# Second MLP of a three-stage kernel: when the next span's block sums are formed, in what pieces they are split, and where the common sum is added

## Chip, cores and metric

One core of a Trainium2 chip. The metric is the device time of one execution in microseconds; where several executions of a kernel are compared, their median is taken.

## What is computed

Attention over a packed set of keys, then two MLPs on 4,608 tokens of 512 features; the change is in the second MLP alone. Cut to that:

```python
def _moe2_ref(x, w_in, w_out):          # x 4608 x 512, w_in 512 x 2048, w_out 2048 x 512
    h = x @ w_in
    g = h * (1.0 / (1.0 + np.exp(-1.702 * h)))
    return (g @ w_out).astype(np.float32)
```

## The kernel before

All matrix products of the second MLP are done in fp32 accuracy by pairs: each operand is split into a high part (a rounded copy, made by ACT) and a low part (operand minus high part, a subtraction on DVE or POOL), and three products stand for one (high x high, high x low, low x high).

**Spans.** The tokens are worked through in five spans: three of 2 x 512 tokens and two of 2 x 384. A span is an up and a down product, each done as a two-by-two block product with seven block products in place of eight (Strassen's scheme in Winograd's form). Its price is sums of blocks. The four blocks of x are b11, b12, b21, b22, each 128 partitions x 2 x 512 (or 384) elements; the block operands of the seven products are b11, t1 = b12 - b11, t2 = b22 - t1, t3 = b22 - b12, b21, b22 and t4 = b21 - t2.

**Groups and steps.** The hidden features of a span are worked in four groups; a group has 14 up steps (two halves of seven, in the order a11, s1, s2, s3, a12, s4, a22, with the x operands b11, t1, t2, t3, b21, b22, t4) and 7 down steps. `up(c)` is an up step: six matmuls into a PSUM bank (line 1051), then the additions that make the activations: `u2` starts as a copy of the a11 product (ACT, line 1062), line 1064 adds the s2 product, line 1066 (called v5 below) adds u2 and the s1 bank, line 1071 adds the s3 product, line 1073 adds u2 to the s4 and the a22 products, and ACT applies the activation (line 1074). There are four banks: a11 and a12 share one (a12 accumulates onto what a11 left), s1 and s4 share one, s3 and a22 share one, s2 has its own. So s4 may be written only when v5 has read the bank, a22 only when line 1071 has, and the next s1 only when line 1073 has taken s4.

`form(d)` makes a down operand: sums of activations on DVE (lines 1087 to 1091), a cast `oh` on ACT (line 1095) and a subtraction `ol` on POOL (line 1096). `down(d)` is a down step: 24 matmuls (18 for 384 tokens) in two parts (line 1122), then additions of the PSUM parts to `acc` or to the common sum `accu` (lines 1147 and 1149). Steps 0 and 1 go to the common sum. In the last group of a span, three quarters of `acc` get the common sum added (line 1153), on POOL, all three behind step 1; the output goes out behind steps 5 and 6.

**Hand-over.** The splits of the x blocks lie in seven tiles with one buffer each. In the last group of a span, behind the second half's product that used a tile last, `prepare` refills it for the next span (called from `up`): a cast on ACT (line 935) and a subtraction (line 936) of the whole block, 1,024 or 768 columns; before or after it the sums of blocks in place, on DVE (lines 1024, 1028, 1029 and 1031). The raw blocks are loaded by `load_x` (line 930) from step 6 of the third group on, into buffers of their own. I call the four changes of span hand-over 1 to 4.

**What sets the order.** The program is written step by step, as above, but a scheduler lays out each engine's queue ahead of time: an instruction may stand earlier than in the text as soon as its operands and buffers are free in the scheduler's own count. Each engine then runs its queue strictly in order, and SP issues the DMAs in order.

## Time and profile before

| | |
|---|---|
| median of 3 executions | 1658.5 us (1656.1 to 1660.7) |
| the profiled execution | 1658.6 us, span 1656.7 us |
| busy: TensorE, DVE, ACT, POOL | 97%, 70%, 52%, 56% of the span |
| matmuls | 10,608 |
| granted clock of TensorE, mean | 0.992 of full speed |

The second MLP takes the part of the span from about 923 us on. TensorE is the engine that the rest serves; the other engines' idle time costs nothing as long as TensorE does not wait for them. The profile names for each idle stretch of an engine what ended it.

### The profile page before, as it was taken

How to read it: one execution, taken by the hardware profiler on the slowest of the kernel's cores; microseconds unless marked ns; L12 is line 12 of the kernel's file. 1: busy time of each engine (PE TensorE's matmuls, PEld its weight loads, DVE VectorE, ACT ScalarE, POOL GpSimd, SP SyncE). 2: the span in 40 equal slices, each digit the busy share in tenths (PEclk: the TensorE clock that was granted, in tenths of full speed). 3: DMA queues.
4: the chain of work that ended last, by engine and by line, in shares of the span. 5: the costliest groups of instructions: out<-in, count | busy, mean ns of one | idle time of the engine just before them, and what ended most of it. 6: DMA issues, size and time to landing. Idle time of an engine off the chain costs nothing.

```text
span 1656.7 us, 29176 instructions
## 1 busy us (share of the span) xinstructions
PE 1611.8 (97%) x10608; PEld 1516.4 (92%) x10608; DVE 1161.9 (70%) x2004; ACT 866.7 (52%) x1771; POOL 928.8 (56%) x744
## 2 busy tenths in 40 slices
PE   7899999999999999999999999999999999999997
PEld 5689998999999999999999889899989999999997
DVE  5788988877768777686886476864585458567564
ACT  4667776666566666665655344434344434434432
POOL 2447777656666557562665266564456446546444
PEclk8999999999999999999999999999999999999999
DMA  9655666584565855465445878676667667887874
GB/s 256 178 163 173 205 189 221 190 254 150 167 204 204 271 186 186 148 207 205 167 177 175 293 259 268 218 245 187 188 207 242 192 186 243 281 250 237 286 222 127
DMA packets 217726, 348.21 MB, mean 210 GB/s; under 512 B 93936, under 2 KB 123632, under 8 KB 211440
## 3 DMA queue, kind: packets, MB, share of 16 engines
q1 hardware_dynamic: 217584, 346.35, 65.1%
q8 instruction: 85, 1.39, 0.3%
q14 instruction: 57, 0.47, 0.1%
HBM read 279.19 MB, written 67.11 MB: 209 GB/s over the span
## 4 chain that ended last, share of the span: by engine, by line
PE 77%; DVE 11%; issue 3%; POOL 3%; DMA 3%; ACT 3%; SPq 0%; POOLq 0%; DVEq 0%; ACTq 0%
PE ps_dn L1122 18%; PE ps_up L1051 18%; PE ps_o L748 15%; PE ps_g L712 13%; PE ps_w L679 3%; PE ps_at L308 3%; PE ps_at L353 2%; PE ps_at L297 2%; PE ps_at L443 2%; DMA vn<-in_v_dram 1%; DVE x_t L936 1%; DVE Wl L684 1%; DVE w L131 1%; POOL Hl L734 0%; DVE between L128 0%
## 5 line engine op out<-in xcount | busy, mean ns | idle before, releaser
L1096 POOL TENSOR_TENSOR ol<-g,oh 128x1024 fp32r<-128x1024 f32 (+1 forms) x120 | 267.2, 2237 | 310.4 <-ACT oh L1095 305.2
L1122 PE MATMUL ps_dn<-wo,oh 128*128 128x256 f32 x2016 | 368.3, 284 | 2.3 <-ACT oh L1095 1.3
L1122 PEld LDWEIGHTS ps_dn<-wo,oh 128*128 128x128 f32 x2016 | 319.9, 192 | 10.2 <-ACT oh L1095 2.0
L748 PE MATMUL ps_o<-Hh,wo 128*128 128x384 f32 x1152 | 321.5, 340 | 2.8 <-ACT Hh L733 1.2
L1122 PE MATMUL ps_dn<-wo,ol 128*128 128x256 f32 x1008 | 278.9, 285 | 3.3 <-POOL ol L1096 3.3
L712 PE MATMUL ps_g<-Aqh,Wh 128*128 128x288 f32 x768 | 232.6, 303 | 6.0 <-DVE th L722 1.5
L712 PE MATMUL ps_g<-Aql,Wh 128*128 128x288 f32 x768 | 226.1, 295 | 0.0
L712 PE MATMUL ps_g<-Aqh,Wl 128*128 128x288 f32 x768 | 225.6, 295 | 0.0
L1051 PE MATMUL ps_up<-x_t,wi 128*128 128x512 f32 (+1 forms) x936 | 215.0, 369 | 7.3 <-DVE g L1073 6.0
L748 PEld LDWEIGHTS ps_o<-Hh,wo 128*128 128x128 f32 x1152 | 210.0, 188 | 8.0 <-ACT Hh L733 2.0
L734 POOL TENSOR_TENSOR Hl<-th,Hh 128x576 fp32r<-128x576 f32 x96 | 139.3, 1452 | 134.4 <-ACT Hh L733 134.1
L748 PE MATMUL ps_o<-Hl,wo 128*128 128x384 f32 x576 | 194.6, 338 | 1.4 <-POOL Hl L734 1.3
L1122 PEld LDWEIGHTS ps_dn<-wo,ol 128*128 128x128 f32 x1008 | 190.7, 193 | 4.4 <-POOL ol L1096 3.7
L1051 PEld LDWEIGHTS ps_up<-x_t,wi 128*128 128x128 f32 x936 | 165.8, 188 | 27.2 <-DVE g L1073 7.1
L684 DVE TENSOR_TENSOR Wl<-ps_w,Wh 64x512 fp32r<-64x512 f32 x192 | 131.7, 686 | 73.1 <-ACT Wh L683 70.6
L1074 ACT ACTIVATE g<-g 128x512 f32<-128x512 f32 (+1 forms) x120 | 70.3, 589 | 206.8 <-DVE g L1071 114.2
L763 POOL TENSOR_TENSOR acc<-acc,add 128x384 f32<-128x384 f32 x135 | 139.0, 1041 | 53.9 <-ACT add L761 52.8
L1095 ACT CAST oh<-g 128x1024 fp32r<-128x1024 f32 (+1 forms) x120 | 113.5, 961 | 103.4 <-PE ps_dn L1122 70.8
L1051 PE MATMUL ps_up<-x_b,wi 128*128 128x512 f32 (+1 forms) x702 | 164.4, 368 | 0.0
L712 PEld LDWEIGHTS ps_g<-Aqh,Wh 128*128 128x128 f32 x768 | 144.0, 188 | 12.0 <-DVE th L722 1.8
L1149 DVE TENSOR_TENSOR acc<-acc,ps_dn 128x512 f32<-128x512 f32 (+1 forms) x160 | 99.2, 630 | 77.9 <-PE ps_dn L1122 73.2
L683 ACT CAST Wh<-ps_w 64x512 fp32r<-64x512 f32 x192 | 111.4, 580 | 78.7 <-PE ps_w L679 46.4
(203 smaller groups left out, 3363.0 us busy)
## 6 DMA issues: line engine op xcount, KB each, us to landing
wo<-wo SPq DMA_DIRECT2D x188, 512.0 KB, 3.9
wi<-wi SPq DMA_DIRECT2D x274, 256.0 KB, 3.7
wg<-wg SPq DMA_DIRECT2D x48, 1024.0 KB, 6.2
raw<-in_moe_w_out_dram SPq DMA_DIRECT2D x28, 512.0 KB, 4.3
wi<-stage SPq DMA_DIRECT2D x24, 512.0 KB, 3.6
wo<-stage SPq DMA_DIRECT2D x24, 512.0 KB, 3.6
x<-acc SPq DMA_DIRECT2D x32, 288.0 KB, 3.4
vn<-in_v_dram SPq DMA_DIRECT2D x16, 512.0 KB, 7.2
```

The lines of the kernel that those rows point to most:

```text
L683: nc.scalar.copy(Wh[rows, :, g], src)
L684: nc.vector.tensor_sub(Wl[rows, :, g], src, fl(Wh[rows, :, g]))
L712: nc.tensor.matmul(ps, st[:, o, g, c * P : (c + 1) * P], mv[:, g, cols], start=n == 0, stop=n == 3 * NG - 1)
L734: nc.gpsimd.tensor_sub(Hl, th, fl(Hh))
L748: nc.tensor.matmul(ps, st[:, m * P : (m + 1) * P], mv[:, cols], start=n == 0, stop=n == 3 * len(ss) - 1)
L763: nc.gpsimd.tensor_add(a, a, t)
L1051: nc.tensor.matmul(o, w[:, y, k], x[:, z, k], start=i == 0 and not go_on, stop=i == 5, skip_group_check=bool(go_on))
L1074: nc.scalar.activation(gf, o if q == "a12" else gf, AF.Gelu_apprx_sigmoid)
L1095: nc.scalar.copy(oh, src)
L1096: nc.gpsimd.tensor_sub(ol, src, fl(oh))
L1122: nc.tensor.matmul(o[:, r], x[:, a, (r0 + r) * P : (r0 + r + 1) * P], w[:, a, y], start=i == 0 and not go_on, stop=i == 6 * m - 1, skip_gr ...
L1149: nc.vector.tensor_add(z, z, o[:, :m])
```

## The change

- `sums` is new. It forms t1 into a tile of its own (`xt`, one buffer), t3 in place of b12, and t2 into two 512-column tiles (tag `w`), at steps given in a table: t1 at step 10 and t3 at step 13 of the third group, t2 at step 2 of the fourth. The fourth sum, t4, stays behind the split of b21.
- `prepare` splits each block in two pieces of 512 (384) columns, cast and subtraction in turn, where it did the whole block at once.
- The three additions of the common sum are behind down steps 2, 3 and 4, one each, and on DVE in the last span.

```diff
@@ -1014,21 +1014,35 @@
                         xr[q] = t[:, :, :n]
                         load_part(xr[q], i0, t0 + k * n, n)
 
-            def prepare(s, q):
+            def sums(s, q):
 
                 if s == len(spans):
                     return
                 n = spans[s][1]
-                b11, b12, b21, b22 = (xr[x] for x in ("b11", "b12", "b21", "b22"))
-                if q == "t2":
-                    nc.vector.tensor_sub(b11, b22, b11)
-                source = {"t1": "b11", "t2": "b11", "t3": "b12", "t4": "b21"}.get(q, q)
-                split_x(q, xr[source], nc.gpsimd if q in ("b11", "b21", "b22") else nc.vector, n)
-                if q == "b11":
-                    nc.vector.tensor_sub(b11, b12, b11)
-                    nc.vector.tensor_sub(b12, b22, b12)
-                elif q == "b21":
-                    nc.vector.tensor_sub(b21, b21, b11)
+                if q == "t1":
+                    xr[q] = wp.tile([P, 2, TH], F32, tag="xt", name="xr", bufs=1)[:, :, :n]
+                    nc.vector.tensor_sub(xr[q], xr["b12"], xr["b11"])
+                elif q == "t3":
+                    nc.vector.tensor_sub(xr["b12"], xr["b22"], xr["b12"])
+                else:
+                    xr[q] = [cv.tile([P, TH], F32, tag="w", name="xr", bufs=2)[:, :n] for _ in range(2)]
+                    for k in range(2):
+                        nc.vector.tensor_sub(xr[q][k], xr["b22"][:, k], xr["t1"][:, k])
+
+            def prepare(s, q):
+
+                if s == len(spans):
+                    return
+                n = spans[s][1]
+                src = xr[{"t3": "b12", "t4": "b21"}.get(q, q)]
+                t = x_tile(q, n)
+                for k in range(2):
+                    part = src[k] if q == "t2" else src[:, k]
+                    nc.scalar.copy(t[:, 0, k], part)
+                    (nc.gpsimd if q[0] == "b" else nc.vector).tensor_sub(t[:, 1, k], part, fl(t[:, 0, k]))
+                if q == "b21":
+                    for k in range(2):
+                        nc.vector.tensor_sub(src[:, k], src[:, k], xr["t2"][k])
 
             g, bank, u2 = {}, {}, {}
 
@@ -1147,10 +1161,10 @@
                         nc.scalar.copy(z, o[:, :m])
                     else:
                         nc.vector.tensor_add(z, z, o[:, :m])
-                if last and j == 1:
-                    for k, c in ((1, 1), (0, 1), (1, 0)):
-                        z = acc[k][:, :per, c * HALF : (c + 1) * HALF]
-                        nc.gpsimd.tensor_add(z, z, acc["u"][:, :per])
+                if last and 2 <= j <= 4:
+                    k, c = ((0, 1), (1, 1), (1, 0))[j - 2]
+                    z = acc[k][:, :per, c * HALF : (c + 1) * HALF]
+                    (nc.vector if s + 1 == len(spans) else nc.gpsimd).tensor_add(z, z, acc["u"][:, :per])
                 if last and j >= 5:
                     k = j - 5
                     for r0, m in parts:
@@ -1163,6 +1177,7 @@
                 load_wi(c)
             for d in range(WOB):
                 load_wo(d)
+            EARLY = {10: "t1", 13: "t3", 16: "t2"}
             form_at, down_at = {}, {}
             for d in range(7 * len(turns)):
                 t, j = divmod(d, 7)
@@ -1175,8 +1190,11 @@
                     load_wi(c + WIB)
                     if c >= 7:
                         next(later, None)
-                    if c % PER == 6 and turns[ups[c][0]][1] == NGR - 2:
-                        load_x(turns[ups[c][0]][0] + 1)
+                    s, at = turns[ups[c][0]][0], (turns[ups[c][0]][1] - NGR + 2) * PER + c % PER
+                    if at == 6:
+                        load_x(s + 1)
+                    elif at in EARLY:
+                        sums(s + 1, EARLY[at])
                 for d in form_at.get(c, ()):
                     form(d)
                 for d in down_at.get(c, ()):
```

Where the instructions stand. First DVE around hand-over 1, from the last sum of the block t4 to the first addition of the next group. `xr` are raw blocks and their sums, `x_t` and `x_b` split blocks, `g` and `s` activations, `u` the tile u2. Before:

```order
L1031 TENSOR_TENSOR xr<-xr 128x1024 [waits Pool_49]
L1073 TENSOR_TENSOR g<-u_13359,ps_up 128x512 [waits PE_49] x2
L1149 TENSOR_TENSOR acc_12402<-acc_12402,ps_dn 128x2x256 [waits PE_49]
L936 TENSOR_TENSOR x_t_13532<-xr,x_t_13532 128x1024 [waits Activation_49]
L1087 TENSOR_TENSOR s_13539<-g 128x1024 [waits Activation_49]
L1149 TENSOR_TENSOR acc_12402<-acc_12402,ps_dn 128x2x256 [waits PE_49]
L1088 TENSOR_TENSOR g<-g 128x1024 [waits DVE_49]
L1089 TENSOR_TENSOR g<-s_13539,g 128x1024 [waits DVE_49,Pool_49]
L1149 TENSOR_TENSOR accu<-accu,ps_dn 128x512 [waits PE_49] x2
L1064 TENSOR_TENSOR u_13586<-u_13586,ps_up 128x512 [waits PE_49,Activation_49]
```

and with the change:

```order
L1024 TENSOR_TENSOR xr<-xr 128x1024 [waits DMAHW7_49,DMAHW1_49,DMAHW0_49]
L1087 TENSOR_TENSOR g<-u_13366,ps_up 128x512 [waits PE_49] x2
L1042 TENSOR_TENSOR x_t_13549<-xr,x_t_13549 128x512 [waits Activation_49] x2
L1163 TENSOR_TENSOR acc_12402<-acc_12402,ps_dn 128x2x256 [waits PE_49]
L1101 TENSOR_TENSOR s_13558<-g 128x1024 [waits Activation_49]
L1163 TENSOR_TENSOR acc_12402<-acc_12402,ps_dn 128x2x256 [waits PE_49]
L1102 TENSOR_TENSOR g<-g 128x1024 [waits DVE_49]
L1103 TENSOR_TENSOR g<-s_13558,g 128x1024 [waits DVE_49,Pool_49]
L1163 TENSOR_TENSOR accu<-accu,ps_dn 128x512 [waits PE_49] x2
L1026 TENSOR_TENSOR xr<-xr 128x1024 [waits DMAHW6_49,DMAHW0_49]
L1030 TENSOR_TENSOR xr<-xr 128x512 x2
L1078 TENSOR_TENSOR u_13605<-u_13605,ps_up 128x512 [waits PE_49,Activation_49]
```

Line 1024 (t1 of the span after next) now stands ahead of line 1087 (1073 before), and line 1026 and the two of line 1030 (its t3 and t2) ahead of line 1078 (1064 before); they wait for block loads of that span. The same holds at hand-overs 2 and 3 (at 3 ahead of line 1103). The block sums of the next span itself are gone from this place.

The sums for hand-over 1 do stand in the third group of the first span, on DVE, second half of the group. Before:

```order
L1064 TENSOR_TENSOR u_12971<-u_12971,ps_up 128x512 [waits PE_49,Activation_49]
L1066 TENSOR_TENSOR g<-u_12971,ps_up 128x512 [waits DVE_49]
L1149 TENSOR_TENSOR acc_12402<-acc_12402,ps_dn 128x2x256 [waits PE_49] x2
L1071 TENSOR_TENSOR g<-g,ps_up 128x512 [waits DVE_49,PE_49]
L1149 TENSOR_TENSOR acc_12401<-acc_12401,ps_dn 128x2x256 [waits PE_49] x2
```

and with the change:

```order
L1078 TENSOR_TENSOR u_12971<-u_12971,ps_up 128x512 [waits PE_49,Activation_49]
L1080 TENSOR_TENSOR g<-u_12971,ps_up 128x512 [waits DVE_49]
L1163 TENSOR_TENSOR acc_12402<-acc_12402,ps_dn 128x2x256 [waits PE_49]
L1024 TENSOR_TENSOR xr<-xr 128x1024 [waits DMAHW6_49,DMAHW7_49,DMAHW4_49,DMAHW3_49]
L1163 TENSOR_TENSOR acc_12402<-acc_12402,ps_dn 128x2x256 [waits PE_49]
L1026 TENSOR_TENSOR xr<-xr 128x1024 [waits DMAHW1_49,DMAHW0_49,DMAHW2_49,DVE_49,Pool_49]
L1030 TENSOR_TENSOR xr<-xr 128x512
L1030 TENSOR_TENSOR xr<-xr 128x512 [waits Pool_49]
L1085 TENSOR_TENSOR g<-g,ps_up 128x512 [waits PE_49]
L1163 TENSOR_TENSOR acc_12401<-acc_12401,ps_dn 128x2x256 [waits PE_49] x2
```

The four subtractions stand between line 1080 and line 1085 (1066 and 1071 before), the first of them behind two block loads, the second behind the third.

Last, POOL at the end of the program. Before:

```order
L1096 TENSOR_TENSOR ol<-g,oh 128x2x384 [waits PE_49,Activation_49] x4
L1096 TENSOR_TENSOR ol<-s_19502,oh 128x2x384 [waits PE_49,Activation_49]
L1096 TENSOR_TENSOR ol<-g,oh 128x2x384 [waits PE_49,Activation_49]
L1153 TENSOR_TENSOR acc_18577<-acc_18577,accu 128x3x256 [waits DMAHW5_49,DMAHW4_49,DVE_49]
L1153 TENSOR_TENSOR acc_18576<-acc_18576,accu 128x3x256 [waits DMAHW1_49,DMAHW0_49]
L1153 TENSOR_TENSOR acc_18577<-acc_18577,accu 128x3x256
L1096 TENSOR_TENSOR ol<-g,oh 128x2x384 [waits PE_49,Activation_49] x2
```

and with the change:

```order
L1110 TENSOR_TENSOR ol<-s_19259,oh 128x2x384 [waits PE_49,Activation_49]
L1110 TENSOR_TENSOR ol<-g,oh 128x2x384 [waits PE_49,Activation_49]
L1110 TENSOR_TENSOR ol<-g,oh 128x2x384 [waits DVE_49,PE_49,Activation_49]
L1110 TENSOR_TENSOR ol<-g,oh 128x2x384 [waits PE_49,Activation_49] x4
L1110 TENSOR_TENSOR ol<-s_19578,oh 128x2x384 [waits PE_49,Activation_49]
L1110 TENSOR_TENSOR ol<-g,oh 128x2x384 [waits PE_49,Activation_49] x3
```

The three additions of line 1153 are gone from POOL's queue; the last two `ol` follow the others at once. On DVE they are line 1167, two of them between the two parts of down step 2's additions, the third ahead of those of step 4:

```order
L1105 TENSOR_TENSOR g<-g 128x2x384 [waits Pool_49]
L1163 TENSOR_TENSOR accu<-accu,ps_dn 128x256 [waits DVE_49,PE_49]
L1163 TENSOR_TENSOR acc_18652<-acc_18652,ps_dn 128x2x256 [waits PE_49]
L1167 TENSOR_TENSOR acc_18652<-acc_18652,accu 128x3x256 [waits DVE_49]
L1167 TENSOR_TENSOR acc_18653<-acc_18653,accu 128x3x256
L1163 TENSOR_TENSOR acc_18652<-acc_18652,ps_dn 128x256 [waits PE_49]
L1163 TENSOR_TENSOR acc_18653<-acc_18653,ps_dn 128x2x256 [waits PE_49]
L1163 TENSOR_TENSOR acc_18653<-acc_18653,ps_dn 128x256 [waits PE_49]
L1167 TENSOR_TENSOR acc_18653<-acc_18653,accu 128x3x256 [waits DVE_49]
L1163 TENSOR_TENSOR acc_18653<-acc_18653,ps_dn 128x2x256 [waits DVE_49,PE_49]
```

## Rows read from the trace of the kernel before

**Rows 1.** The waits of TensorE: who waited for whom, us in total, times, longest.

```profile
PE ps_up L1051 <- DVE g L1073: 6.0, 3, 2.4
```

**Rows 2.** Timeline, hand-over 1: start us, us, engine line op out<-in xcount [idle before <-releaser].

```profile
1046.78 1.23 DVE L1028 TENSOR_TENSOR xr<-xr 128x1024 f32<-128x1024 f32 x1
1047.14 3.13 POOL L1096 TENSOR_TENSOR ol<-g,oh 128x1024 fp32r<-128x1024 f32 x1 [0.40 <-ACT oh L1095]
...
1048.04 3.31 DVE L1029 TENSOR_TENSOR xr<-xr 128x1024 f32<-128x1024 f32 x1
...
1065.97 1.27 DVE L1073 TENSOR_TENSOR g<-u,ps_up 128x512 f32<-128x512 f32 x2
...
1066.70 1.66 PE L1051 MATMUL ps_up<-x_t,wi 128*128 128x512 f32 x6 [2.41 <-DVE g L1073]
```

**Rows 3.** Timeline, first span, third group, its second half.

```profile
1010.26 1.96 SPq L930 DMA_DIRECT2D xr<-x  x4
...
1013.73 0.69 DVE L1071 TENSOR_TENSOR g<-g,ps_up 128x512 f32<-128x512 f32 x1 [0.70 <-PE ps_up L1051]
...
1016.89 2.41 POOL L1096 TENSOR_TENSOR ol<-g,oh 128x1024 fp32r<-128x1024 f32 x1 [5.04 <-ACT oh L1095]
...
1019.15 1.52 PE L1051 MATMUL ps_up<-x_t,wi 128*128 128x512 f32 x6
```

**Rows 4.** The tile of the raw blocks and sums, its loads: issue to landing.

```profile
DMA to landing us min/median/max: 2.6/4.1/7.3
```

**Rows 5.** 512-column subtractions on DVE and POOL, and ACT's cast: ns min/median/max, first and last start.

```profile
L957 DVE TENSOR_TENSOR x_t<-x_t,x_t x6: 684/842/1389, 790.5 to 850.2; 128x512 fp32r<-128x512 f32 x6
...
L906 POOL TENSOR_TENSOR stage<-sums,stage x16: 1284/1292/1568, 360.0 to 1001.4; 128x512 fp32r<-128x512 f32 x16
...
L955 ACT CAST x_t<-x_t x6: 611/614/621, 784.7 to 848.8; 128x512 fp32r<-128x512 f32 x6
```

**Rows 6.** Timeline behind hand-over 1, the next span's first group.

```profile
1070.44 0.94 SPq L930 DMA_DIRECT2D xr<-x  x2
...
1071.95 1.22 DVE L1089 TENSOR_TENSOR g<-s,g 128x1024 f32<-128x1024 f32 x1
...
1073.21 2.00 ACT L1095 CAST oh<-g 128x1024 fp32r<-128x1024 f32 x2 [4.50 <-DVE g L1089]
...
1073.81 1.52 PE L1051 MATMUL ps_up<-x_b,wi 128*128 128x512 f32 x6
1074.29 0.68 DVE L1064 TENSOR_TENSOR u<-u,ps_up 128x512 f32<-128x512 f32 x1
1074.34 4.77 POOL L1096 TENSOR_TENSOR ol<-g,oh 128x1024 fp32r<-128x1024 f32 x2 [9.38 <-ACT oh L1095]
...
1079.07 2.40 POOL L1096 TENSOR_TENSOR ol<-s,oh 128x1024 fp32r<-128x1024 f32 x1
```

**Rows 7.** Timeline, TensorE at hand-overs 2 and 4.

```profile
1226.80 1.42 PE L1051 MATMUL ps_up<-x_t,wi 128*128 128x512 f32 x5 [2.40 <-DVE g L1073]
...
1510.25 0.97 PE L1051 MATMUL ps_up<-x_t,wi 128*128 128x384 f32 x4 [1.18 <-DVE g L1073]
```

**Rows 8.** Timeline of the tail.

```profile
1634.89 2.25 DVE L1091 TENSOR_TENSOR g<-g 128x768 f32<-128x768 f32 x1
...
1638.81 5.42 POOL L1153 TENSOR_TENSOR acc<-acc,accu 128x768 f32<-128x768 f32 x3
...
1646.04 0.58 PE L1122 MATMUL ps_dn<-wo,ol 128*128 128x256 f32 x1 [2.84 <-POOL ol L1096]
```

**Rows 9.** The chain of waits at its end: start us, us, what.

```profile
1646.04 6.31 PE ps_dn L1122 x28
```

**Rows 10.** Busy time by stretch: length, PE to POOL busy (xcount), PEclk, DMA share, GB/s.

```profile
1040.00:1095.00 55.00, 52.59 (x327) 47.20 (x326) 42.62 (x43) 24.15 (x30) 35.28 (x14) 1.00 0.69 218
1638.00:1641.00 3.00, 3.00 (x28) 3.00 (x27) 0.72 (x3) 0.90 (x2) 3.00 (x3) 1.00 0.53 165
1646.00:1649.00 3.00, 2.96 (x14) 2.96 (x15) 0.35 (x1) 0.00 (x0) 1.77 (x1) 0.50 0.00 0
```

## The prediction

> **What bounds the kernel now.** I read the waits of TensorE first, then the timelines around the four hand-overs from one span to the next, then the tail. In the second MLP TensorE hardly waits: 6.0 us in three places on DVE's line 1073 [rows 1], and once for 2.84 us on POOL's `ol` in the tail [rows 8]. So the change can win back those waits and what hangs on them, no more; any new wait of TensorE is paid in full.
>
> The waits on line 1073 come from DVE being late at a hand-over. In hand-over 1, DVE forms the sums and the splits of the next span's blocks. The 1,024-column subtraction takes 1.23 us at 1046.78; the next one takes 3.31 us, because POOL's `ol`, started at 1047.14, sits beside it [rows 2]. The row reads as taking turns: `ol` begins in earnest when the first subtraction ends (1048.0), runs 2.3 us to 1050.3, and only then does the second run its 1.1 us, to 1051.35. Were the two to share evenly, the second would end near 1050.3. The Trainium skill (SBUF — State Buffer, section Who interferes with whom) says the same more strictly: a VectorE instruction with two SBUF inputs and a GpSimd instruction that reads SBUF lock each other out for a whole instruction. I use turns below. DVE reaches line 1073 at 1065.97, and TensorE, which needs that bank for the first `t1` product, starts at 1066.70 after 2.41 us idle [rows 2].
>
> **The change, part by part.** The order of the changed program decides this, and it does not put the sums where the table EARLY names them. For hand-over 1 they stand in the third group. For hand-overs 2 to 4 they stand right after the hand-over before: the buffers are free by then, so `t1` moves ahead of the addition to `g` on which TensorE waits, and `t3` and the two pieces of `t2` ahead of the addition to `u2`.
>
> 1. *Third group of the first span.* The four last block loads go out between 1010.26 and 1012.2 [rows 3]; b12's second piece, near 1011.2, lands 4.1 us later at the median [rows 4], 1015.3. `t1` then ends at 1016.5 and an accumulation at 1017.1. `t3` meets `ol` (1016.89 to 1019.30) [rows 3] and ends at 1020.4; two pieces of `t2`, 0.68 us each alone [rows 5], end near 1021.7, and the addition of s3, which stood at 1013.73, ends near 1022.4. The a22 product writes onto the bank that this addition reads, and stood at 1019.15 [rows 3]; the new order puts five down matmuls (0.6 us) ahead of it. **+2.6**, bounds 0 (all loads landed early) and +3.3.
>
> 2. *Hand-over 1, the old wait.* Out go three subtractions, 1.2, 3.3 and 1.2 us. In come 512-column pieces, 0.68 us on DVE, 1.29 on POOL [rows 5]. In turns: the split of `t3` ends at 1056.4; the first piece of `t4` waits for POOL's second b21 piece (1058.9), ends at 1059.5; an accumulation; the second piece waits for an `ol` (to 1061.9), ends at 1062.5; the next span's `t1`, now in this place, waits for a piece of b22 (1063.7) and ends at 1064.9, where line 1073 stood at 1065.97. **-1.1**, bounds -2.4 (the wait gone) and 0.
>
> 3. *Hand-over 1, a new wait.* Counted on with this 1.1 us: `t4` split to 1067.4, the three sums of the activations to 1072.0, two `accu` additions to 1073.2. Now come `t3`, `t2`, `t2` for the next span, and only then `u2` and the addition v5 behind it. b22's load is queued on SP behind b21's, which waits for the split of `t4`; so its second piece is issued near 1069.8 (1070.44 to 1071.38 before), and lands near 1074. But POOL has three `ol` in a row here: the casts started at 1073.21 when line 1089 was done, and POOL ran from 1074.34 through 1081.47 without a gap [rows 6]. Moved up with DVE they start near 1073.2. In turns: `t3` 1075.5 to 1076.6; `ol`; a piece, 1078.9 to 1079.6; `ol`; a piece, 1081.8 to 1082.4; `u2` 1083.0; v5 1083.6, which ended near 1075.7 before (`u2` began at 1074.29, and two such additions take 0.7 each). TensorE's s4 product goes onto the bank that v5 reads. It is through with what stands ahead of it (b21's product, 1.1 us before the 1073.81 of [rows 6] and 1.4 long, the first matmuls of two down steps, then 20 waiting on `ol`) near 1077.9. **+5.8** on s4, and +0.6 on `ol`. Bounds: +2.4 if `t3` gets in ahead of the first `ol`, +8 if b22 lands after the second `ol` began. By even sharing it would be +1.3.
>
> 4. *Hand-over 2* repeats this with 768-column sums; its old wait is the same 2.40 [rows 7]. Here b22's load is one transfer, landing near the moment DVE is free, so `t3` may get in first: 2.8 us of wait, else 5.6. **-1.1 + 4.5**, bounds -2.4 + 2.8 and 0 + 6.6.
>
> 5. *Hand-over 3.* It had no wait. Its sums stand ahead of line 1103 (1089 before), so what they take (0.95 and two of 0.55 by the columns, 2.1 us) and a wait for b22 delay the casts behind it. **+2**, bounds 0 and +4.
>
> 6. *Hand-over 4* has no next span: the sums are gone and nothing takes their place. Its wait of 1.18 [rows 7] goes: **-1.2**, bounds 0 and -1.6.
>
> 7. *The tail.* POOL's three additions of the common sum, 5.42 us from 1638.81, stand ahead of the last two `ol`; TensorE waits 2.84 us, to 1646.04 [rows 8]. It then runs its last 28 matmuls in 6.31 us [rows 9], at a granted clock of 0.50, the lower of its two levels (1.2 GHz of 2.4), where 28 took 3.00 us at 1.00 [rows 10]. In the new order the additions are DVE's. They take turns with three `ol`, as line 1091 does in its 2.25 us [rows 8] for some 0.9 of work: the first ends at 1639.7, the second at 1642.4. The second part of step 4's bank is freed behind it, 1642.8 where TensorE wants it at 1641.1, 1.7 us of new wait. Steps 4 to 6 then end at 1647.8 instead of 1652.4. **-4.6**, bounds -6.3 (no such wait) and -2.8 (the clock falls all the same).
>
> 8. *The clock after new waits.* After 2.41 us of idling in hand-over 1 the granted clock stayed 1.00; in the tail, after 2.84 us, it was 0.50 [rows 10]. A wait of 5.8 us is over both, so I add what half speed costs for a few us after the resumption: **+2.5** over the two places, bounds 0 and +6. The Trainium skill (TensorE: Matmul & The Clock Gate, section HAM oscillation) has every long enough gap in matmul work paid again in slow matmuls behind it; by that alone all three new waits would pay, near +6, by the row of hand-over 1 none.
>
> Costed at nothing: ACT's copies in halves (0.62 us each [rows 5], a quarter of a microsecond more for each block; the products that need them come seven up steps later, and without that cover it would be 0.25 x 7 at each hand-over) and POOL's additions at the other four ends, no longer in one block of 7 us; TensorE did not wait there.
>
> Sum: 2.6 - 1.1 + 5.8 + 0.6 - 1.1 + 4.5 + 2 - 1.2 - 4.6 + 2.5 = **+10.0**. The profiled execution took 1658.6 us (span 1656.7), 0.1 above the median of 1658.5, so 1668.5.
>
> **The rivals.**
> *The sums ride free.* The scheduler put them there because DVE was idle in its own count. If DVE gets to `t3` before the casts are done and b22 has landed by then, v5 is in time. It hangs on one race: b22's landing (2.6 to 7.3 us in [rows 4]) against the first `ol` of the group. Then terms 1, 3, 5 and 8 are nought, and -1.1 - 1.1 - 1.2 - 4.6 = -8.0: 1650.6; with every wait of [rows 1] gone, about 1647. For it: the row of line 1089 and the casts are only 1.3 us apart, so a little less delay wins the race. Against: three `ol` back to back in [rows 6], and a load that cannot go out before `t4` is split.
> *Small waits.* The new waits stay at their lower bounds (2.4 and 2.8) and the clock does not fall: -1.1 + 2.4 + 0.6 - 1.1 + 2.8 - 1.2 - 4.6 = -2.2, up to +2 with part of term 1: 1656 to 1661. For it: even sharing, which [rows 2] speak against.
> *The change does not do what its words say*: for three of four hand-overs the sums are not in the third group. That is in the forecast already.
>
> **How the numbers follow.** Forecast, new waits dearer than the old: 0.54. Riding free: 0.27. Small waits: 0.19. About 0.3% (5.0 us) is what a measurement can tell from no change. So slower 0.54, same 0.19, faster 0.27. The likeliest case by itself runs from 1663.5 to 1681 (upper bounds of 1, 3, 4 and 8). The range reaches down to the riding case, 1650, and up to 1680.
>
> **What would show it.** Right: TensorE waits of 2 us and more on DVE's line 1080 soon after hand-overs 1 and 2; DVE's lines 1026 and 1030 there at two to three times their own length; a wait on line 1085 in the first span's third group; no wait on POOL in the tail, and full clock to the end. Wrong: no TensorE wait on line 1080, or DVE waiting nowhere for block loads; then the time falls to 1651. If the tail still shows half clock, term 7 is oversized by 1.8.

## The result and the profile after

| | |
|---|---|
| before, median of 6 executions | 1658.58 us (1656.10 to 1661.33) |
| after, median of 6 executions | 1669.47 us (1667.53 to 1671.82) |
| after over before | 1.0066, 95% interval 1.0052 to 1.0080 |
| the profiled execution after | 1668.5 us, span 1666.7 us |
| busy after: TensorE, DVE, ACT, POOL | 97%, 70%, 52%, 56% of the span |

The change made the kernel 10.9 us slower. The shares of busy time are the same as before, to the per cent; what changed is in the waits of TensorE over the second MLP (who waited for whom, us in total, times, longest), which answer to [rows 1] (the list is of all of them but one of 0.7 us at the start):

```profile
PE ps_dn L1136 <- DVE accu L1163: 8.2, 2, 7.5
PE ps_up L1065 <- DVE g L1080: 5.3, 1, 5.3
PE ps_up L1065 <- DVE g L1085: 3.6, 2, 2.3
PE ps_dn L1136 <- ACT oh L1109: 2.3, 2, 1.4
PE ps_dn L1136 <- DVE acc L1163: 1.4, 1, 1.4
PE ps_up L1065 <- DVE g L1087: 1.1, 2, 0.7
PE ps_dn L1136 <- POOL ol L1110: 1.0, 2, 0.6
```

The old wait, 6.0 us on line 1073, is down to 1.1 us (line 1087 now). In its place stand one of 7.5 us on an addition to the common sum (hand-over 2), one of 5.3 us on v5 (line 1080, hand-over 1) and one of 2.3 us on line 1085 (third group of the first span). The second wait in four of these groups stood before the change too: 0.8 us on the common sum, 0.9 on `oh` and 0.4 on `ol` in the tail, and 1.3 us on the addition of s3 near 955 us.

To see where the time went, I take one instruction that both kernels run 80 times, DVE's addition of u2 to g (line 1073 before, 1087 after), and compare the starts of the same one in the two profiled executions:

| stretch, from and to a start of that addition before / after | forecast | measured |
|---|---|---|
| all ahead of the change's first place: to 1002.49 / 1000.17 | 0 | -2.3 |
| third group of the first span: to 1041.85 / 1042.15 | +2.6 | +2.6 |
| hand-over 1: to 1119.24 / 1125.58 | +6.6 | +6.0 |
| hand-over 2: from 1201.96 / 1208.31 to 1300.22 / 1314.82 | +4.7 | +8.3 |
| hand-over 3: to 1431.98 / 1448.01 | +2.0 | +1.4 |
| hand-over 4: to 1565.41 / 1579.24 | -1.2 | -2.2 |
| tail: from 1625.72 / 1639.54 to the span's end | -4.6 | -3.8 |
| sum | +10.0 | +10.0 |

(The forecast's 2.5 us for the clock are shared out evenly over hand-overs 1 and 2; the rows are rounded.) The first row is no effect of the change, whose queues are the same up to there: at the same addition the other kernels below stood between 4.7 us earlier and 1.4 us later than before's.

*Third group*, timeline (start us, us, engine line op, idle before and its releaser):

```profile
1013.49 1.23 DVE L1024 TENSOR_TENSOR xr<-xr 128x1024 f32<-128x1024 f32 x1 [4.22 <-DMA xr<-x]
...
1014.58 2.41 POOL L1110 TENSOR_TENSOR ol<-g,oh 128x1024 fp32r<-128x1024 f32 x1 [5.20 <-ACT oh L1109]
...
1015.23 2.83 DVE L1026 TENSOR_TENSOR xr<-xr 128x1024 f32<-128x1024 f32 x1
1017.99 1.28 DVE L1030 TENSOR_TENSOR xr<-xr 128x512 f32<-128x512 f32 x2
1019.19 0.68 DVE L1085 TENSOR_TENSOR g<-g,ps_up 128x512 f32<-128x512 f32 x1
...
1019.92 1.66 PE L1065 MATMUL ps_up<-x_t,wi 128*128 128x512 f32 x6 [2.34 <-DVE g L1085]
```

DVE waits 4.22 us for a block load, does four sums, one of them beside an `ol`, and only then the addition of s3 that frees the bank for a22.

*Hand-over 1*, timeline behind it, the answer to [rows 6]:

```profile
1072.97 5.72 POOL L1110 TENSOR_TENSOR ol<-g,oh 128x1024 fp32r<-128x1024 f32 x2 [7.23 <-ACT oh L1109]
...
1074.44 2.01 DVE L1026 TENSOR_TENSOR xr<-xr 128x1024 f32<-128x1024 f32 x1 [1.44 <-DMA xr<-x]
1076.37 5.61 DVE L1030 TENSOR_TENSOR xr<-xr 128x512 f32<-128x512 f32 x2
...
1078.65 2.78 POOL L1110 TENSOR_TENSOR ol<-s,oh 128x1024 fp32r<-128x1024 f32 x1
...
1082.62 0.69 DVE L1080 TENSOR_TENSOR g<-u,ps_up 128x512 f32<-128x512 f32 x1
...
1083.36 2.93 PE L1065 MATMUL ps_up<-x_b,wi 128*128 128x512 f32 x6 [5.29 <-DVE g L1080]
```

The two pieces of `t2`, 1.28 us together in the third group, take 5.61 us here: one `ol` goes before each of them. TensorE stands from 1078.07 to 1083.36.

*Hand-over 2*, the same place:

```profile
1238.86 5.40 POOL L1110 TENSOR_TENSOR ol<-g,oh 128x1024 fp32r<-128x1024 f32 x2 [7.22 <-ACT oh L1109]
...
1238.94 3.12 DVE L1026 TENSOR_TENSOR xr<-xr 128x768 f32<-128x768 f32 x1 [0.66 <-DMA xr<-x]
1241.98 5.30 DVE L1030 TENSOR_TENSOR xr<-xr 128x384 f32<-128x384 f32 x2
1247.21 0.68 DVE L1163 TENSOR_TENSOR accu<-accu,ps_dn 128x512 f32<-128x512 f32 x1
...
1247.94 0.80 PE L1136 MATMUL ps_dn<-wo,oh 128*128 128x256 f32 x2 [7.45 <-DVE accu L1163]
```

`t3` came 0.08 us behind the `ol`, and here an addition to the common sum stands behind the sums too, so TensorE stopped at that bank.

*The clock* behind the two waits, and in the tail (by stretch: length, PE to POOL busy (xcount), granted clock, DMA share, GB/s), against [rows 10]:

```profile
1084.00:1086.00 2.00, 2.00 (x6) 1.60 (x5) 2.00 (x4) 1.57 (x2) 0.00 (x0) 0.50 0.00 0
...
1250.00:1252.00 2.00, 2.00 (x12) 2.00 (x11) 1.73 (x2) 0.63 (x1) 0.00 (x0) 0.50 0.03 8
...
1655.00:1659.00 4.00, 2.60 (x21) 2.61 (x22) 3.86 (x6) 0.00 (x0) 2.71 (x2) 1.00 0.00 0
```

Half speed behind both waits, full speed to the end in the tail, where before it was 0.50.

### The profile page after: what moved, and what is told of

The parts are those of the page before. It is cut to its first block, busy times and chain, and to the rows that moved or that the text cites. A ratio compares the mean times of both kernels' runs of the same rounds, so it can differ in the third digit from the quotient of the medians.

```text
span 1666.7 us, 29225 instructions
## 1 busy us (share of the span) xinstructions
PE 1609.4 (97%) x10608; PEld 1515.7 (91%) x10608; DVE 1171.9 (70%) x2031; ACT 873.0 (52%) x1799; POOL 927.1 (56%) x753
## 4 chain that ended last, share of the span: by engine, by line
PE 79%; DVE 9%; DMA 4%; ACT 3%; issue 3%; POOL 2%; SPq 1%; DVEq 0%; ACTq 0%; POOLq 0%
PE ps_dn L1136 19%; PE ps_up L1065 18%; PE ps_o L748 15%; PE ps_g L712 14%; PE ps_w L679 3%; PE ps_at L308 3%; PE ps_at L353 2%; PE ps_at L297 2%; PE ps_at L443 1%; DMA vn<-in_v_dram 1%; DVE xr L1030 1%; DVE Wl L684 1%; DMA xr<-x 1%; DVE x_t L1042 1%; POOL Hl L734 1%
```

## The experiments

Every median below stands against the kernel before, run in turn with it on the same chip, whose median was 1659.6 to 1660.1 us there; ratios are to that, with their 95% intervals. Differences between medians of different experiments are across such series.

**1. The tail's edit alone.** Before, with

```diff
-                if last and j == 1:
-                    for k, c in ((1, 1), (0, 1), (1, 0)):
...
+                if last and 2 <= j <= 4:
+                    k, c = ((0, 1), (1, 1), (1, 0))[j - 2]
...
+                    (nc.vector if s + 1 == len(spans) else nc.gpsimd).tensor_add(z, z, acc["u"][:, :per])
```

> The kernel before, with the third part of the change alone: the three additions of the common sum apart, on DVE in the last span. Sums and splits of the blocks stay as they were. Forecast's theory: the additions on POOL ahead of the last two ol cost a wait of 2.84 us and half speed behind it, so this part alone gives what the tail of the changed kernel shows, 3.8 us less from the last activations to the end: 1654.8 (1653.5 to 1656). The profile shows no wait of 2.8 us on ol in the tail and a granted clock of 1.00 to the end. Rival, the tail gained because everything ahead of it was late and left POOL and DVE in another state: this part alone gives under 1 us, 1657.6 to 1658.6.

Measured: 1655.34 us, 0.9967 (0.9957 to 0.9978). In the tail no wait of 2.8 us on `ol` is left; the longest (waits of TensorE in the tail) is one on step 4's bank:

```profile
PE ps_dn L1122 <- DVE acc L1149: 1.4, 1, 1.4
```

From the last addition of u2 to g to the span's end it takes 27.15 us, before 30.98, after 27.14. So the tail's gain is this edit's own, 3.8 us. The run also showed something that I hadn't asked for: at hand-over 1, where nothing differs from before, the same wait of 2.41 us was followed by half speed here, and not in before's profile [rows 10]. Timeline, and the stretch behind:

```profile
1066.22 2.60 PE L1051 MATMUL ps_up<-x_t,wi 128*128 128x512 f32 x6 [2.41 <-DVE g L1073]
```

```profile
1067.00:1069.00 2.00, 2.00 (x7) 1.63 (x6) 2.00 (x3) 1.23 (x3) 0.00 (x0) 0.50 0.94 288
```

**2. The pieces alone.** Before, with the split of every block in two halves:

```diff
-                split_x(q, xr[source], nc.gpsimd if q in ("b11", "b21", "b22") else nc.vector, n)
+                src, t = xr[source], x_tile(q, n)
+                for k in range(2):
+                    nc.scalar.copy(t[:, 0, k], src[:, k])
+                    (nc.gpsimd if q[0] == "b" else nc.vector).tensor_sub(t[:, 1, k], src[:, k], fl(t[:, 0, k]))
```

> The kernel before, with the second part alone: every split of a block goes in 512- (384-)column pieces, the sums stay whole and in their old places at the hand-over, the common sum stays on POOL. Forecast's theory (turns with ol): a piece locks DVE out for a shorter stretch and starts as soon as its half of the cast is there, so the old waits on DVE's line that frees the bank for t1 (2.41, 2.40 and 1.18 us) shrink by about a half, to 1.2 each at most: 1655.5 (1654 to 1657.5). Rival, pieces only add instructions (six more subtractions on DVE and eight more casts at each hand-over, each with its fixed part of a few hundredths to a tenth of a us) and each piece takes a turn of its own with ol, so DVE is as late or later: 1658.6 to 1662.

Measured: 1655.24 us, 0.9968 (0.9957 to 0.9980), as the theory had it. Of the waits on DVE's line (6.0 us before) 1.1 us are left at the hand-overs, but `oh` on ACT takes part of their place (2.5 us, 0.4 before; waits of TensorE from 1040 to 1540):

```profile
PE ps_dn L1125 <- ACT oh L1098: 2.5, 6, 0.7
PE ps_up L1054 <- DVE g L1076: 1.1, 1, 1.1
```

That is 2.8 us. Measured by stretches as above, hand-overs 1 and 2 are 1.3 us shorter each, 3 and 4 are 0.3 and 0.1 longer: 2.2 us less in all. The tail, which this kernel does not touch, was 1.0 us shorter (29.97 us): half speed began 1.3 us after TensorE resumed there and lasted 3.4 us, where before it held over nearly all of the 6.3 us of the last matmuls [rows 9]. So the profiled pair accounts for 3.2 of the 4.5 us, and a third of that is the clock's and not the edit's.

**3. The sums held where the table names them.** The changed kernel, with the sums pinned behind what is written ahead of them:

```diff
-                    nc.vector.tensor_sub(xr[q], xr["b12"], xr["b11"])
+                    tc.keep_in_program_order(nc.vector.tensor_sub(xr[q], xr["b12"], xr["b11"]))
...
-                    nc.vector.tensor_sub(xr["b12"], xr["b22"], xr["b12"])
+                    tc.keep_in_program_order(nc.vector.tensor_sub(xr["b12"], xr["b22"], xr["b12"]))
...
-                        nc.vector.tensor_sub(xr[q][k], xr["b22"][:, k], xr["t1"][:, k])
+                        tc.keep_in_program_order(nc.vector.tensor_sub(xr[q][k], xr["b22"][:, k], xr["t1"][:, k]))
```

> The changed kernel, with the four sums held in program order on DVE, so that they stand where the table names them: t1 behind the s3 addition of the third group's second half, t3 at its end, the two pieces of t2 in the fourth group behind v5. Pieces and tail stay changed. Forecast's theory (the new waits come from the place of the sums ahead of u2, v5 and the common sum, while three ol run): the waits of 5.3 us on v5 and 7.5 us on the common sum's addition behind hand-overs 1 and 2 are gone, and with them the half speed behind each (1.5 and 2.9 us) and the 1.4 us behind hand-over 3: 1669.5 - 18.6 = 1650.9, and up to 2.3 us more at each of three hand-overs if t1 in the third group holds up a bank: 1650 to 1657. Rival, the waits come from the work itself (pieces and sums are more than DVE can do beside ol, wherever they stand): waits of 3 us and more turn up in the third and fourth groups, 1663 to 1670.

Measured: 1645.56 us, 0.9916 (0.9902 to 0.9931), and 1645.64 in a later series. Between 1000 and 1600 us the view lists no wait of TensorE at all. What is left are the two waits ahead of the change's first place, as before, and those of the tail, these two the longest there:

```profile
PE ps_dn L1136 <- DVE acc L1163: 1.4, 1, 1.4
PE ps_dn L1136 <- ACT oh L1109: 1.1, 1, 1.1
```

The rival falls: DVE can do all of it, in another place. The turns are paid there too: in the fourth group, beside two `ol`, the two pieces of `t2` take 4.62 us, and they hold TensorE up nowhere.

```profile
1031.82 4.62 DVE L1030 TENSOR_TENSOR xr<-xr 128x512 f32<-128x512 f32 x2
```

This is 23.9 us faster than the changed kernel and about 14 us faster than the kernel before, the version that beats both. I had expected 18.6 us, and the time lies below my range (1650 to 1657). The third group's 2.3 us and the 1.7 us of waits on line 1087 and on `ol` at hand-overs 1 and 2, which I had left standing, go as well; for the other 1.3 us I have no row.

**4. One input in place of two.** The changed kernel, with `t3` and `t2` as passes over one block; it leaves their subtraction out.

```diff
-                    nc.vector.tensor_sub(xr["b12"], xr["b22"], xr["b12"])
+                    nc.vector.tensor_reduce(xr["b12"], xr["b22"].rearrange("p k (n o) -> p k n o", o=1), axis=AX.X, op=ALU.add)
...
-                        nc.vector.tensor_sub(xr[q][k], xr["b22"][:, k], xr["t1"][:, k])
+                        nc.vector.tensor_reduce(xr[q][k], xr["b22"][:, k].rearrange("p (n o) -> p n o", o=1), axis=AX.X, op=ALU.add)
```

> The changed kernel, with the sums t3 and t2 put in the same places of the same queues as a pass that reads one block only (a reduction over an axis of length one, 128x1024 and 128x512); the subtraction is left out. All other instructions and their order are the same. It asks whether turns with POOL's ol, by the second SBUF input, make the price of the new place. Forecast's theory: without a second input DVE and ol run side by side, so behind hand-over 1 t3 ends 1.2 us after its block landed and the two pieces 1.3 us later, u2 and v5 end some 4.5 us earlier than in the changed kernel: the wait on v5 falls from 5.3 to under 1.5 us, the one on the common sum's addition from 7.5 to under 3, the clock stays at 1.00 behind the first of them: 1669.5 - 4.5 - 1.5 - 4.5 - 2 = 1657 (1655 to 1660). Rival, DVE and POOL slow each other whatever the operands (or the late landing of the block is what counts): the pieces still take 2 us and more, waits of 4 us and more remain, 1666 to 1670.

Measured: 1651.81 us, 0.9949 (0.9932 to 0.9966). Timeline behind hand-over 1, beside that of the changed kernel above:

```profile
1072.13 4.75 POOL L1110 TENSOR_TENSOR ol<-g,oh 128x1024 fp32r<-128x1024 f32 x2 [7.23 <-ACT oh L1109]
...
1073.32 1.22 DVE L1026 TENSOR_REDUCE xr<-xr 128x1024 f32<-128x1024 f32 x1 [1.17 <-DMA xr<-x]
1074.46 1.27 DVE L1030 TENSOR_REDUCE xr<-xr 128x512 f32<-128x512 f32 x2
...
1075.65 0.68 DVE L1078 TENSOR_TENSOR u<-u,ps_up 128x512 f32<-128x512 f32 x1
...
1076.36 0.69 DVE L1080 TENSOR_TENSOR g<-u,ps_up 128x512 f32<-128x512 f32 x1
...
1076.84 2.41 POOL L1110 TENSOR_TENSOR ol<-s,oh 128x1024 fp32r<-128x1024 f32 x1
...
1077.75 2.58 DVE L1105 TENSOR_TENSOR g<-g 128x1024 f32<-128x1024 f32 x1
```

The sums stand at the same places of the same queues here (in the third group the two pieces stand ahead of `t3`, and not behind it): the two pieces take 1.27 us beside an `ol`, not 5.61, and the two `ol` 4.75 us, not 5.72. v5 starts 3.0 us after `t3` does, not 8.2. TensorE's waits on v5 (5.3 us) and in the third group (2.3 us) are gone, the one on the common sum is 0.7 us (7.5). So turns with `ol` set the price of the new place. That it is the second SBUF input, and not the kind of instruction that was put in, the other rows of this run bear out: line 1078, a sum with one operand in SBUF and one in PSUM, takes 0.68 us while `ol` runs, and line 1105, a sum with both in SBUF, takes 2.58 us beside the third `ol` (1.22 in the changed kernel, where POOL was idle then). The Trainium skill (SBUF — State Buffer, section Who interferes with whom) has a reduction on Trainium2 as an operation that never contends with GpSimd, and a sum of two SBUF operands as one that does; the two runs agree, with 1.27 and 5.61 us. The time, 1651.81, lies below my range (1655 to 1660): I had left the third group's 2.3 us standing and allowed up to 3 us on the common sum. What is left at hand-over 3, 1.5 us on `oh`, comes of no turns: there the sums take their own 0.96 and 1.02 us in the changed kernel as well, and merely stand ahead of the casts.

**5. Whole blocks, sums pinned.** Experiment 3 with

```diff
-                for k in range(2):
-                    part = src[k] if q == "t2" else src[:, k]
-                    nc.scalar.copy(t[:, 0, k], part)
...
+                else:
+                    nc.scalar.copy(t[:, 0], src)
+                    (nc.gpsimd if q[0] == "b" else nc.vector).tensor_sub(t[:, 1], src, fl(t[:, 0]))
```

> The kernel of the pinned sums (1645.6), with its splits of whole blocks again, as before the change (t2 alone stays in two pieces, since it lies in two buffers). Theory: the pieces and the place of the sums pay for the same thing, DVE's lateness at the hand-over. DVE reached the line that frees the bank for t1 at 1065.97 before and was wanted at 1064.3; with three sums of 1.2 us gone from the hand-over it is there by 1062.5 with whole splits too, so the pieces are worth nothing more: 1645.6 to 1647. Rival: the pieces are worth by themselves what they were worth alone, 4.5 us: 1649 to 1651, with waits of 1 us and more at the hand-overs.

Measured: 1648.76 us (1644.39 to 1649.84), 0.9925 (0.9909 to 0.9941). Three waits come back at the hand-overs, none as long as 1 us (the same view):

```profile
PE ps_up L1068 <- DVE g L1090: 1.6, 3, 0.6
```

Above experiment 3 it is 3.2 us by the medians, 1.5 by the ratios, whose intervals overlap. By stretches of the two profiled executions the four hand-overs take 0.9, 1.0, 0.4 and 0.7 us more, 3.0 in all, where the pieces alone (experiment 2) gave 2.2. So the theory that the pieces are worth nothing beside pinned sums falls: one execution of each shows the two parts of the edit adding up, and not paying for the same lateness.

**6. The tail's additions on POOL, apart.** Experiment 3 with

```diff
-                    (nc.vector if s + 1 == len(spans) else nc.gpsimd).tensor_add(z, z, acc["u"][:, :per])
+                    nc.gpsimd.tensor_add(z, z, acc["u"][:, :per])
```

> The kernel of the pinned sums, with the three additions of the common sum on POOL in the last span too, apart behind steps 2, 3 and 4 as in the change. It asks which half of the tail's edit pays: apart, or DVE. Theory: DVE. POOL's queue then has ol, two additions (1.8 us each), ol, an addition, ol; the last ol ends 11 us after the first of the three begins at 1628.3, at 1639.3, where TensorE wants it at 1637.3: the wait of 1.43 us on DVE's acc goes, one of 2 to 2.8 us on ol comes, and with it, in part of the executions, half speed for 3.4 us and more (1.7 us): 1646 to 1649. Rival: apart is what pays, since no block of 5.4 us stands ahead of an ol: 1644 to 1645.5.

Measured: 1648.48 us, 0.9933 (0.9921 to 0.9946), 2.9 us above experiment 3 by the medians. The wait on `ol` is back (waits in the tail), with half speed behind it (the stretch 1637 to 1640):

```profile
PE ps_dn L1136 <- POOL ol L1110: 1.9, 1, 1.9
```

```profile
1637.00:1640.00 3.00, 2.36 (x11) 2.09 (x11) 1.95 (x4) 0.00 (x0) 1.86 (x2) 0.50 0.44 167
```

DVE is what pays in the tail; apart on POOL the tail is 30.37 us long, nearly before's.

**7. The tail's order.** Experiment 3, with the three additions of the last span pinned behind both parts of the step they follow; then both kernels once more, side by side.

```diff
-                    (nc.vector if s + 1 == len(spans) else nc.gpsimd).tensor_add(z, z, acc["u"][:, :per])
+                    i = (nc.vector if s + 1 == len(spans) else nc.gpsimd).tensor_add(z, z, acc["u"][:, :per])
+                    if s + 1 == len(spans):
+                        tc.keep_in_program_order(i)
```

> The kernel of the pinned sums, with the three additions of the common sum in the last span held in program order on DVE: each stands behind both parts' additions of the step it follows, where the scheduler had put two of them ahead of the second part's addition of step 2. Theory (the forecast's term for the tail: step 4's bank is freed behind them): the wait of 1.43 us on DVE's acc in the tail goes: 1644.1 (1643.8 to 1644.8). Rival: DVE has the same work to do before the last step, so the wait only moves to the last additions or to the banks of steps 5 and 6: 1645.2 to 1646.

> The kernel of the pinned sums once more, as the partner of the next run on the same chip: 1645.6 (1644.5 to 1647), with 1.43 us of wait on DVE's acc in the tail.

> The kernel with the tail's additions in program order once more, beside its partner. If the 1.43 us of wait taken away in the tail are worth their length, 1.1 to 1.4 us below the partner. If the scatter of the clock from one execution to the next is larger than that, the two medians lie within 0.6 us of each other and this pair can't tell.

Measured: 1645.75 us; in the pair 1644.74 beside 1645.64, ratios 0.9912 (0.9897 to 0.9927) and 0.9918 (0.9903 to 0.9932). The wait of 1.43 us is gone in both profiles and the tail 1.1 us shorter (26.28 us twice, 27.36 and 27.38 without), so the forecast's mechanism for that wait holds. The medians, one 0.2 us above and one 0.9 below, can't tell it.

**8. The common sum's addition ahead of the sums.** The changed kernel, with

```diff
-                    nc.vector.tensor_sub(xr["b12"], xr["b22"], xr["b12"])
+                    with tc.issue_after(tail_add[s - 2].ins) if s > 1 else nullcontext():
+                        nc.vector.tensor_sub(xr["b12"], xr["b22"], xr["b12"])
...
-                        nc.vector.tensor_add(z, z, o[:, :m])
+                        add = nc.vector.tensor_add(z, z, o[:, :m])
+                        if last and j == 0:
+                            tail_add[s] = add
```

and the same around the pieces of `t2`.

> The changed kernel, with the sums t3 and t2 of the second to fourth hand-over queued on DVE behind both parts' additions of step 0 to the common sum; else as the change has it (at hand-over 1 and the third group nothing moves). It asks why the wait behind hand-over 2 was 7.5 us where the forecast had 5.6 at most and 4.5 as its value. Theory: there one of the two additions to the common sum stood behind the sums, so TensorE stopped at that bank 1.6 us after t3 had begun, before the twenty matmuls that it still had ahead of s4 at hand-over 1; with the addition ahead of the sums the wait goes to v5 and comes down to that of hand-over 1 or below, 4.5 to 6 us, and at hand-over 3 the 1.4 us on oh go, with 0 to 3 us on v5 in their place: 1669.5 - 2.2 - 0.5 = 1667 (1664 to 1668.5). Rival: the race with the first ol and the turns behind it set the end whatever stands first, TensorE waits 7 us and more in all at hand-over 2: 1668.5 to 1671.

Measured: 1669.22 us (1664.84 to 1674.58), 1.0066 (1.0045 to 1.0086): by the median no better than the change, and spread over 9.7 us, the change over 4.3. The profile showed 3.1 us of wait at hand-over 2, not 7.5; but `t3` had also begun 0.05 us ahead of the `ol`. So each of the two kernels was profiled in one more execution.

> The same kernel as in the run with the common sum's addition ahead of the sums, another execution, for its profile: there t3 at hand-over 2 began 0.05 us ahead of the first ol, where in the changed kernel it began 0.08 us behind it, so the order and the race are not told apart. If t3 loses the race here: by the theory (the order of the addition set the extra length) TensorE waits 4.5 to 6 us on v5 at hand-over 2 and nowhere on the common sum; by the rival (the race alone) 7 us and more in all. If it wins again, 3 us in all, and the question stays open.

> The changed kernel, another execution, for its profile. If t3 at hand-over 2 wins the race against the first ol here, with the common sum's addition still behind the sums: by the theory TensorE waits 5 us and more on that addition (the sums are 0.95, 2.4 beside an ol and 2.4, then the addition, 1.6 us after TensorE ran dry); by the rival 3 us. If it loses again, 7.5 us as before, and the wait's length is seen to repeat. The waits of 2.3 us in the third group and 5.3 us at hand-over 1 are expected again within 0.3 us; the stretches of half clock behind them may differ.

These two single executions took 1671.62 and 1668.18 us. `t3` lost its race in the first and won it in the second. At hand-over 2 the timeline (`t3` on DVE and the first `ol` on POOL) and the waits of TensorE (1240 to 1260) of the second profile of the changed kernel:

```profile
1241.10 0.96 DVE L1026 TENSOR_TENSOR xr<-xr 128x768 f32<-128x768 f32 x1 [0.30 <-DMA xr<-x]
...
1241.36 5.55 POOL L1110 TENSOR_TENSOR ol<-g,oh 128x1024 fp32r<-128x1024 f32 x2 [7.21 <-ACT oh L1109]
```

```profile
PE ps_dn L1136 <- DVE accu L1163: 5.0, 1, 5.0
```

Of experiment 8, first profile (`t3` is line 1029 there, v5 line 1084, `ol` line 1114):

```profile
1242.01 0.95 DVE L1029 TENSOR_TENSOR xr<-xr 128x768 f32<-128x768 f32 x1
...
1242.06 5.81 POOL L1114 TENSOR_TENSOR ol<-g,oh 128x1024 fp32r<-128x1024 f32 x2 [7.21 <-ACT oh L1113]
```

```profile
PE ps_up L1069 <- DVE g L1084: 1.8, 1, 1.8
PE ps_dn L1140 <- POOL ol L1114: 1.3, 1, 1.3
```

And its second profile:

```profile
1242.34 5.46 POOL L1114 TENSOR_TENSOR ol<-g,oh 128x1024 fp32r<-128x1024 f32 x2 [7.22 <-ACT oh L1113]
...
1242.42 3.13 DVE L1029 TENSOR_TENSOR xr<-xr 128x768 f32<-128x768 f32 x1
```

```profile
PE ps_up L1069 <- DVE g L1084: 4.8, 1, 4.8
PE ps_dn L1140 <- POOL ol L1114: 0.6, 1, 0.6
```

Together with the changed kernel's first profile that is a full table of TensorE's wait at hand-over 2:

| | `t3` ahead of the `ol` | `t3` behind it |
|---|---|---|
| common sum's addition behind the sums (the change) | 5.0 us | 7.5 us |
| addition ahead of the sums | 3.1 us | 5.4 us |

The race is worth 2.3 to 2.5 us, the order 1.9 to 2.1, and they add. By the stretch of hand-over 2, the clock included, the four stand 5.4 and 8.3, 3.1 and 6.1 us above before, in the order of the table. Each cell is one execution; the 5.3 us at hand-over 1 came again in all four. That the medians don't show the gain is no contradiction: at hand-over 3 this order costs 3.0 us of waits where the change has 1.4 or 1.5 (the stretch is 3.2 us above before, and not 1.4), and half speed behind the many waits differs from one execution to the next.

## Why the prediction was right

Forecast: 1668.5 us, slower, from +10.0. Measured: 1669.47, the profiled pair 9.9 us apart. By its steps:

1. *Third group, +2.6*: 2.6, wait of 2.34 us on line 1085. `t1` began at 1013.49, 1015.8 on the clock of before, where I had the load land at 1015.3, and `t3` met the `ol` as described.
2. *Old wait, -1.1 at hand-overs 1 and 2*: 0.7 and 0.4 us are left of 2.41 and 2.40, so -1.7 and -2.0. A little undersized. The waits that I read were those on line 1073 and one on `ol` alone; the view has 1.3 us on `oh` as well, 0.4 of it at hand-over 4 (step 6), and 0.8 on the common sum in the tail.
3. *Hand-over 1, new wait, +5.8 and +0.6 on `ol`*: 5.29 and 0.57 us. The chain was right step by step, turns included; experiment 4 shows that the turns are the cause, experiment 3 that the place is.
4. *Hand-over 2, +4.5*: the step that was mis-sized. It measured 7.45, above my upper bound of 6.6, and not on line 1080 but on line 1163. I had carried over hand-over 1 and asked only whether `t3` would win its race (2.8 or 5.6). Those two values hold for a DVE queue with both additions to the common sum ahead of the sums (3.1 and 5.4 in experiment 8). At hand-over 2 the order has one of them behind, and that is another 2 us.
5. *Hand-over 3, +2*: +1.4, a wait of 1.4 us on `oh`, by the mechanism given.
6. *Hand-over 4, -1.2*: -2.2. I had counted the wait on line 1073 and not the one of 0.4 us on `oh` behind it; for the other 0.6 I have no row.
7. *Tail, -4.6*: TensorE's last matmul ends 22.3 us behind the last addition of u2 to g, before 26.6, so -4.4, with 1.42 us of new wait on step 4's bank (1.7) and full clock. The end behind it is 0.5 us longer, so -3.8 in all. Experiments 1, 6 and 7 bear each part of it out.
8. *Clock, +2.5*: the row of hand-over 1 before (2.41 us of wait, full clock) was one draw. In after's profile half speed held TensorE up from 1083.4 to about 1086.5 and from 1247.9 to about 1253.7, 8.9 us in all, of which a half, 4.4, is lost: undersized, within its bounds. The Trainium skill (TensorE: Matmul & The Clock Gate, section HAM oscillation) says that each long enough gap is paid again in slow matmuls; the two long waits agree with it, the short ones go either way (below).

Hand-over 2 came out 3.6 us dearer than forecast; the 2.3 us that the profiled execution gained ahead of the change by chance, hand-over 4 and the smaller terms made up for it in that pair. In the second profile of the changed kernel, where `t3` won its race at hand-over 2, the stretches of the change sum to +9.6 us, where those of the first give +12.3. So part of the closeness is luck. The signs of the eight steps are not, nor are their places, but for hand-over 2: there TensorE stood at the bank of the common sum and not at that of s4.

Three slips in the prediction's sums touch neither the forecast nor the order of the rivals: riding free with every wait of line 1073 gone comes to 1648 and not 1647; *small waits* reaches +2 only with more than term 1's bound; and the upper bounds as stated add up to 1678 and not 1681.

Of the rivals, riding free hung on the race of `t3` against the first `ol`. At hand-over 2 `t3` won it in two of four profiles, and TensorE still waited 3.1 and 5.0 us: winning against the first `ol` spares one turn of three. Small waits needed DVE and POOL to share evenly; the rows behind hand-over 1 and experiment 4 rule that out. The sums where the change's own table names them give 1645.6 (experiment 3).

## What to carry to other kernels

Where a scheduler lays out the queues, what a table in the source says of the place of an instruction is a wish: read the order it made, and pin what must not move up. Off the critical path is no licence to put work ahead of a queue's next critical instruction: 2 to 2.5 us of DVE work cost TensorE 5 to 7.5 us, since the two-operand sums in SBUF waited out an `ol` on POOL each; at a place with time to spare the same turns cost it nothing (experiment 3). And when one place is worked out in full, check the order of the next place instruction by instruction before its result is carried over.

## What the runs showed of the hardware that was not expected

- **A start decides a whole turn.** `t3` 0.08 us behind the `ol` took 3.12 us, and 0.05 us ahead of it 0.95 us, with that `ol` then held up instead (3.13 us in place of 2.4). Both orders came up in executions of the same kernel. The record of the instruction that is held up begins at once and contains its waiting.
- **A short gap may or may not cost the clock.** The same 2.41 us at hand-over 1 left the granted clock at 1.00 in before's profile and brought it to 0.50 in experiment 1, where six matmuls took 2.60 us instead of 1.66. Of the third group's wait, 2.34 us in after's profile, the same holds: 1.00 there, and 0.50 in experiment 8 (the stretch behind the wait in each):

```profile
1020.00:1023.00 3.00, 3.00 (x20) 2.74 (x21) 2.30 (x4) 1.16 (x2) 0.00 (x0) 1.00 0.46 142
```

```profile
1022.00:1025.00 3.00, 3.00 (x13) 2.71 (x12) 2.30 (x4) 0.63 (x1) 0.00 (x0) 0.50 0.20 54
```

So a wait of this size is to be priced with a chance of half speed on top, and one profile does not say which it will be.
